# A fused attention and two-layer kernel on one core: another order of the work around the seven products for x w_in

## The chip, the core and the metric

The kernel runs on one core of a Trainium2 chip. The metric is the device time of one execution in microseconds; a kernel's time is the median of its runs. The core has a matrix engine (TensorE, PE in the profile, with its weight loads as PEld), a vector engine (DVE), a scalar engine (ACT), GpSimd (POOL) and SyncE (SP), which here issues all DMA transfers. Each engine works through its own instructions in the order in which the program emits them, and waits on semaphores for the others.

## The reference

Three parts follow each other. q, k, v have 4 batches, 8 heads, 576 rows, 64 columns; the token matrix x that leaves the first part is 2304 x 512, and the weights are 64-bit numbers.

```python
kv = einsum('bhsd,bhse->bhde', k, v)
out = einsum('bhsd,bhde->bhse', q, kv)
x = out / sqrt(mean(out * out, -1) + 1e-6) * g_norm      # as tokens x 512
h = x @ w_in                                             # 512 x 2048
x = (h * sigmoid(h)) @ w_out                             # 2048 x 512
result = ((x @ w_a) * (x @ w_b)) @ w_out2                # 512 x 1536, twice; 1536 x 512
```

## The kernel before, in words

**Tiling.** The 2304 tokens are six blocks j of 384 (TB). A float32 value is held as a high and a low part, and a product is made as three matmuls (high by high, low by high, high by low). w_in and w_out are split into sixteen pieces s of 128 of the inner dimension. PSUM tiles have tags: "h" and "at" with two buffers each, "acc" with four. In SBUF, 37 buffers of 4 KB per partition have the tag "page" and hold weights, raw weights, k and v, and much else; a tile takes a page once an earlier one has had its last use, and a transfer into it waits for that use.

**Steps.** After a start written out by hand (ORDER) the work goes in steps g. VISITS lists which block passes which pieces; base[] is the step at which each visit begins: 0, 4, 12, 20, 28, 32, 48, 64, 80. Steps 4 to 63 are step1: twelve matmuls h = x w_in of one piece (L345), the gate on ACT, its split into gh (ACT) and gl (DVE), then x1_mm, twelve matmuls with w_out (L371) for the step *before*. Blocks 2 and 3 run in steps 32 to 63.

**Work hung on steps.** at(g, f) puts f behind x1_mm of step g, at(-g, f) puts it ahead of those; early[g] puts it between the gate's gh and gl. So the order on every engine is written out through these numbers. On steps 4 to 25 the Decoder turns 64-bit w_in and w_out into high and low parts, with a second key in steps 6 and 9 (EXTRA). Hung on steps are further: sums(u), which makes the additional matrices for the seven products (add, split, store in three steps) and stores them to hsd and hcd; attention of later blocks; combine, which does the same for the x blocks; prepare, which decodes w_a and w_b, forms sums and stores them to wd (twelve calls n, two for each pair p of pieces); and loads.

**Attention items.** For block j and head pair p: load_q_blocks (4 DMAs, 8 where the block crosses a batch, as block 4 does), turn_q (DVE transposes into qT), attend (matmuls ao on PE, squares on ACT, sum on DVE, power on POOL), norm_mul (DVE, xn), and stage_d or stage_f (PE transposes xtp, copies). load_kv and kv_pair make kvc for a batch and a head pair (matmuls kvps). kvps, ao and xtp all use tag "at".

**Units.** From step 64 on, blocks 4 and 5 pass x w_in together: unit u handles pieces 2u and 2u+1 by seven products of six matmuls (L649, Strassen's scheme; banks X, Y, V, Z; the seventh accumulates into Z, so DVE must have read the fifth), with x1_mm calls after products 3 and 6. The first unit has only one x1_mm to do. hooks[k] hold what follows product k+1: what was hung on step 64 + 2u comes at hook 3, on the next step at hook 6; load_unit fetches the matrices of later units (hw 0 to 3 from hsd and hcd). Then sixteen steps (80 to 95) do x1_mm for block 5, during which load_x and load_pairs fetch the transformed x (xc) and the first pairs of w_a, w_b matrices (wp) and raw w_out2. Then eighteen calls of products (seven products with w_a, seven with w_b) alternate with out_mm (L825). decode_out decodes w_out2 in six small parts. load_pairs loads in a fixed order as long as fewer than 21 (NLIVE) matrices are live.

## Time and profile before

| | us |
|---|---|
| median of 3 runs | 893.66 (892.92 to 896.52) |
| profiled execution, its time | 892.13 |
| its span, first to last instruction | 890.3 |
| mean granted TensorE clock | 0.994 |

The profile comes from one execution. Busy time of an engine is the time in which it executed; matmuls are pipelined and their ends modelled. A granted clock of 1.00 is the higher of TensorE's two levels (2.4 GHz), 0.50 the lower (1.2 GHz). A row in a timeline ends with the idle time of the engine before it and with what ended that idle time.

### The profile page before, as it was taken

The numbers are of one execution on the slowest core, as the hardware profiler recorded it, in microseconds if no ns is written. First come the engines' busy times: TensorE is split into PE (matmuls) and PEld (weight loads), VectorE is DVE, ScalarE is ACT, GpSimd is POOL, SyncE is SP. The second block draws the span as 40 slices with busy tenths as digits, with TensorE's granted clock in tenths as the row PEclk, the third lists the DMA queues.
The fourth block names the chain that finished last, engine by engine and source line by source line (L and its number), as shares of the span: only waits on it lengthen the run. The fifth ranks groups of instructions, "written<-read, shape, count | busy, mean of one in ns | idle before, by whom it ended". The sixth has DMA issues, their size and how long they took to land.

```text
span 890.3 us, 13591 instructions
## 1 busy us (share of the span) xinstructions
PE 864.0 (97%) x5014; PEld 819.2 (92%) x5015; DVE 606.1 (68%) x1153; ACT 330.5 (37%) x670; POOL 52.0 (6%) x53
## 2 busy tenths in 40 slices
PE   8999999999999999999989999999999999999998
PEld 5799999999889999999979999999999999999996
DVE  4878998757576786757533878886556665545555
ACT  4766654445254554344422433321131211131110
POOL 4410002001111100000000000000000000000000
PEclk9999999999999999999989999999999999999999
DMA  9950974856885379987599699497777567765001
GB/s 282 376 206 1 276 254 143 264 170 232 251 238 167 140 278 327 340 293 272 213 421 420 269 326 351 151 343 284 272 267 262 179 223 286 266 227 193 1 1 71
DMA packets 124930, 212.19 MB, mean 238 GB/s; under 512 B 41280, under 2 KB 85824, under 8 KB 124864
## 3 DMA queue, kind: packets, MB, share of 16 engines
q1 hardware_dynamic: 124864, 211.33, 67.4%
q8 instruction: 39, 0.64, 0.3%
q14 instruction: 27, 0.22, 0.1%
HBM read 143.92 MB, written 67.37 MB: 237 GB/s over the span
## 4 chain that ended last, share of the span: by engine, by line
PE 78%; DMA 10%; DVE 5%; ACT 2%; issue 1%; SPq 1%; POOL 0%; ACTq 0%; DVEq 0%
PE op L825 17%; PE x1p L371 14%; PE hp L345 11%; PE Z_b L649 4%; PE V_b L649 4%; PE X_b L649 4%; DMA wp<-wd 4%; PE Z_a L649 4%; PE X_a L649 4%; PE V_a L649 4%; PE Y_b L649 2%; PE Y_a L649 2%; PE Z_h L649 2%; DMA hw<-hsd 2%; PE V_h L649 2%; PE X_h L649 2%
## 5 line engine op out<-in xcount | busy, mean ns | idle before, releaser
L371 PE MATMUL x1p<-gh,wo 128*128 128x384 f32 x768 | 197.1, 340 | 4.8 <-ACT gh L355 4.8
L371 PEld LDWEIGHTS x1p<-gh,wo 128*128 128x128 f32 x768 | 140.8, 191 | 5.4 <-ACT gh L355 5.4
L371 PE MATMUL x1p<-gl,wo 128*128 128x384 f32 x384 | 129.5, 341 | 0.4 <-DVE gl L360 0.3
L345 PE MATMUL hp<-xh,wi 128*128 128x384 f32 x512 | 103.5, 343 | 0.4 <-ACT xh L252 0.3
L345 PEld LDWEIGHTS hp<-xh,wi 128*128 128x128 f32 x512 | 88.3, 188 | 1.4 <-ACT xh L252 1.0
L360 DVE TENSOR_TENSOR gl<-g,gh 128x384 fp32r<-128x384 f32 x96 | 54.2, 566 | 46.1 <-ACT gh L355 45.7
L825 PE MATMUL op<-wp,ab 128*128 128x512 f32 x360 | 83.4, 390 | 0.0
L825 PEld LDWEIGHTS op<-wp,ab 128*128 128x128 f32 x360 | 67.5, 188 | 13.6
L706 ACT CAST ab<-a 128x384 fp32r<-128x384 f32 x72 | 37.0, 514 | 115.0 <-DVE a L700 58.3
L371 PEld LDWEIGHTS x1p<-gl,wo 128*128 128x128 f32 x384 | 73.2, 191 | 1.6 <-DVE gl L360 1.6
L833 DVE TENSOR_TENSOR o<-op,o 128x512 f32<-128x512 f32 x90 | 60.5, 686 | 16.6 <-PE op L825 16.6
L825 PE MATMUL op<-w,ab 128*128 128x512 f32 x288 | 66.9, 390 | 0.0
L825 PEld LDWEIGHTS op<-w,ab 128*128 128x128 f32 x288 | 54.0, 188 | 10.9
L355 ACT CAST gh<-g 128x384 fp32r<-128x384 f32 x96 | 49.3, 513 | 22.9 <-PE x1p L371 20.6
L409 ACT ACTIVATE g<-hp 128x384 f32<-128x384 f32 x64 | 31.3, 489 | 67.9 <-PE hp L345 67.9
L345 PE MATMUL hp<-xl,wi 128*128 128x384 f32 x256 | 55.1, 335 | 0.0
L230 POOL TENSOR_TENSOR rr<-ss,nhalf 128x6 f32<-128x6 f32 x24 | 35.8, 1494 | 228.9 <-DVE ss L225 228.9
L345 PEld LDWEIGHTS hp<-xl,wi 128*128 128x128 f32 x256 | 45.3, 188 | 0.3 <-DVE xl L256 0.3
L649 PE MATMUL Z_a<-xc,wp 128*128 128x384 f32 x216 | 43.5, 336 | 1.9 <-DMA xc<-xcd 1.7
L649 PE MATMUL X_a<-xc,wp 128*128 128x384 f32 x216 | 43.7, 337 | 0.0
L649 PE MATMUL Z_b<-xc,wp 128*128 128x384 f32 x216 | 43.3, 335 | 0.0
L649 PE MATMUL V_a<-xc,wp 128*128 128x384 f32 x216 | 43.3, 335 | 0.0
(177 smaller groups left out, 1425.0 us busy)
## 6 DMA issues: line engine op xcount, KB each, us to landing
wp<-wd SPq DMA_DIRECT2D x114, 512.0 KB, 6.7
xc<-xcd SPq DMA_DIRECT2D x21, 768.0 KB, 8.9
hw<-hsd SPq DMA_DIRECT2D x24, 512.0 KB, 6.7
raw_wi<-in_moe_w_in_dram SPq DMA_DIRECT2D x16, 512.0 KB, 8.1
raw_wo<-in_moe_w_out_dram SPq DMA_DIRECT2D x16, 512.0 KB, 7.0
hsd<-hs SPq DMA_DIRECT2D x16, 512.0 KB, 3.8
raw_wa<-in_moe_w_a_dram SPq DMA_DIRECT2D x12, 512.0 KB, 6.3
wd<-s_wa SPq DMA_DIRECT2D x12, 512.0 KB, 3.8
```

Of the source, the lines that this page charges most:

```text
L230: nc.gpsimd.tensor_tensor(r, rms[j, p], nhalf, op=ALU.pow)
L345: nc.tensor.matmul(o, w[wp][:, kt * P:(kt + 1) * P], x[key][:, kt, :], start=(n == 0), stop=(n == 3 * KD - 1))
L355: nc.scalar.copy(gh, src)
L360: nc.vector.tensor_sub(gl, src, gh.bitcast(F32))
L371: nc.tensor.matmul(acc[vi][c], w[wp][:, c * P:(c + 1) * P], gg[vi, s][g], start=(s == s0 and i == 0), stop=(s == s1 - 1 and i == 2))
L409: nc.scalar.activation(g, o, AF.Silu)
L649: nc.tensor.matmul(b[bank], w(name, wq, kt), x(i, xq, kt), start=(fresh and k == 0), stop=(k == 5), skip_group_check=True)
L706: nc.scalar.copy(o[:, 0], t)
L825: nc.tensor.matmul(o, ab[d, p, f, n][:, g, ts], wp[p, 7 + f][:, wq * DM:(wq + 1) * DM], start=(k == 0), stop=(k == 5))
L833: nc.vector.tensor_add(t, o, t)
```

## The change

**Attention.** The items of blocks 3, 4 and 5 come as one list with g0 = 33, 35, ..., 55: block 3 first (four items), then blocks 4 and 5 by turns. Each has load_q_blocks at g0-5, kv load at g0-2 and kv_pair at g0 (not for block 5), turn_q at g0, attend at g0+1, norm_mul ahead of the rest at g0+2, stage_d or stage_f at g0+3. Before, block 3 stood at a pitch of three (34, 37, 40, 43), blocks 4 and 5 at 45, 46, 48, 49, 51, 52, 54, 55. The loads kvt go from steps 32 and 43 to 30 and 38.

**prepare.** Four parts become six: scale (ACT), first_half and second_half (joins on DVE, second also ACT's cast of a), add (stores a, then four sums), high (three ACT casts), low (three DVE subtractions and stores). Calls 0 to 5 begin at steps 36, 42, 48, 54, 58 and 62 with loads three steps ahead, and use side and early places by turns; calls 6 to 11 are spread over the hooks after products 1, 3, 4 and 7 of the units, one part for each, five places apart, loads three places ahead. What call 5 has left over goes to the first three such places.

**Loads and decoding.** decode_out of pair 0 moves from steps 92 and 93 into the first products call (its first half for one piece, its second half for the other). load_pairs takes one load at step 87 and three at each of steps 93 to 95, where it took two at each of 87 to 95. sums(u) begin at 8, 12, 15, 18, 25, 26, 28, 29, before at 11, 14, 17, 20, 24, 26, 28, 30, and store with four DMAs in place of six. combine of blocks 4 and 5 begins one step earlier for kt = 0.

```diff
@@ -262,7 +262,7 @@
         stage_d3(j, p)
 
 
-    raws, mids, W = {}, {}, {}
+    raws, mids, W, wt_ = {}, {}, {}, {}
     srcs = {"wi": w_in, "wo": w_out, "wa": w_a, "wb": w_b, "w2": w_out2}
 
     def load_w(key):
@@ -320,7 +320,7 @@
         dec_sign(key)
 
     def dec_high(key):
-        w = page([P, 2, DM], F32R, f"{key[0]}_{key[1]}")
+        w = wt_[key] = page([P, 2, DM], F32R, f"{key[0]}_{key[1]}")
         nc.scalar.copy(w[:, 0], mids[key])
         W[key] = w[:, 0], w[:, 1]
 
@@ -506,17 +506,20 @@
             for f in wait.pop(0):
                 f()
 
-        def step0():
+        def scale():
             dec_scale(keys[0])
             dec_scale(keys[1])
+
+        def first_half():
             decode(0)
 
-        def step1():
+        def second_half():
             o = page([P, 2, DM], F32R, f"a_{kind}{p}")
             hi(o[:, 0], o[:, 1], m[0], (wd[p, (0, 4)[mat]], flat(o)))
             decode(1)
 
-        def step2():
+        def add():
+            rest()
             for h in range(2):
                 s.append(page([P, 2, DM], F32R, f"s_{h}_{kind}{p}"))
             a11, a12, a21, a22 = (e[:, h * H2:(h + 1) * H2] for e in m for h in range(2))
@@ -525,18 +528,19 @@
             nc.vector.tensor_sub(s3, a11, a21)
             nc.vector.tensor_sub(s2, s1, a11)
             nc.vector.tensor_sub(s4, a12, s2)
-            rest()
-
-        def step3():
+
+        def high():
             a21, a22 = m[1][:, 0:H2].bitcast(F32R), m[1][:, H2:]
             for h in range(2):
                 o = s[h]
                 hi(o[:, 0], o[:, 1], o[:, 1].bitcast(F32), (wd[p, ((1, 2), (5, 6))[mat][h]], flat(o)))
             hi(a21, a22.bitcast(F32R), a22, (wd[p, 3, :, mat * DM:(mat + 1) * DM], m[1].bitcast(F32R)))
+
+        def low():
             for _ in range(3):
                 rest()
 
-        return load, [step0, step1, step2, step3]
+        return load, [scale, first_half, second_half, add, high, low]
 
     w2raw = []
     stores = []
@@ -675,7 +679,7 @@
     PLACES = {"mid": 6, "sig": 2, "gh": 2, "gl": 2}
     ab = {}
 
-    def products(d, p, after=None, more=()):
+    def products(d, p, after=None, more=(), more_b=()):
 
         a = {}
         for n, got in enumerate(seven_ab(d, p, 0, "mid")):
@@ -691,24 +695,26 @@
             if 1 <= n <= len(more):
                 more[n - 1]()
         low = None
-        for got in seven_ab(d, p, 1, "sig"):
+        for n, got in enumerate(seven_ab(d, p, 1, "sig")):
+            if 1 <= n <= len(more_b):
+                more_b[n - 1]()
             if got is None:
                 continue
-            f, n, z, u = got
-            t = a[f, n]
+            f, i, z, u = got
+            t = a[f, i]
             if u is None:
                 nc.vector.tensor_mul(t, z, t)
             else:
-                c = sb.tile([P, TB], F32, tag=("gh", "gl")[f], bufs=2, name=f"b_{d}_{p}_{f}{n}")
+                c = sb.tile([P, TB], F32, tag=("gh", "gl")[f], bufs=2, name=f"b_{d}_{p}_{f}{i}")
                 nc.vector.tensor_add(c, z, u)
                 nc.vector.tensor_mul(t, c, t)
-            o = page([P, 2, TB], F32R, f"ab_{d}_{p}_{f}{n}")
+            o = page([P, 2, TB], F32R, f"ab_{d}_{p}_{f}{i}")
             nc.scalar.copy(o[:, 0], t)
 
             if low:
                 low()
             low = lambda t=t, o=o: nc.vector.tensor_sub(o[:, 1], t, o[:, 0].bitcast(F32))
-            ab[d, p, f, n] = o
+            ab[d, p, f, i] = o
         low()
 
     def sums(u):
@@ -733,9 +739,8 @@
                 nc.vector.tensor_sub(t[:, 1], t[:, 1].bitcast(F32), t[:, 0].bitcast(F32))
 
         def store():
-            for q in range(2):
-                nc.sync.dma_start(hsd[u, 0, :, q * DM:(q + 1) * DM], w0[q].bitcast(F32))
-                nc.sync.dma_start(hcd[u // 2, :, u % 2, q], w1_[q][:, H2:].bitcast(F32))
+            nc.sync.dma_start(hsd[u, 0], wt_["wi", 2 * u].rearrange("p i f -> p (i f)").bitcast(F32))
+            nc.sync.dma_start(hcd[u // 2, :, u % 2], wt_["wi", 2 * u + 1][:, :, H2:].bitcast(F32))
             for h in range(2):
                 nc.sync.dma_start(hsd[u, 1 + h], s[h].rearrange("p i f -> p (i f)").bitcast(F32))
 
@@ -867,26 +872,14 @@
         stage_b(j, p)
         norm_head(j, p)
 
-    for b, g0, pairs in ((2, base[5], (0, 1, 2, 3)), (3, base[5] + 11, (0, 2, 1, 3))):
-        at(g0, load_kvt, b)
-        for i, p in enumerate(pairs):
-            at(g0 + 3 * i, load_kv, b, p)
-            at(g0 + 2 + 3 * i, kv_pair, b, p)
-
     v4 = base[4]
     for p in range(NP):
         at(v4 - 9 + 2 * p, turn_q, 2, p)
         at(v4 - 8 + 2 * p, attend, 2, p)
         at(-(v4 - 7 + 2 * p), norm_mul, 2, p)
         at(v4 + p // 2, stage_d, 2, p)
-    for p in range(NP):
-        at(-(base[5] + 4 + 3 * p), norm_mul, 3, p)
-        at(base[5] + 2 + 3 * p, turn_q, 3, p)
-        at(base[5] + 3 + 3 * p, attend, 3, p)
-        at(base[5] + 5 + 3 * p, stage_d, 3, p)
     for i in range(4):
         at(v4 - 13 + i, load_q_blocks, 2, i)
-        at(base[5] - 4 + i, load_q_blocks, 3, i)
 
     def stage_f(j, p):
         if j not in xf:
@@ -894,23 +887,46 @@
         stage_d1(j, p)
         nc.scalar.activation(xf[j][:, p, :], xt.pop((j, p)), AF.Copy, scale=g2)
 
-    for i, (p, j) in enumerate([(p, j) for p in (0, 2, 1, 3) for j in (4, 5)]):
-        g0 = base[5] + 13 + i * 3 // 2
-        at(g0 - 4, load_q_blocks, j, p)
+    at(base[5] - 2, load_kvt, 2)
+    at(base[5] + 6, load_kvt, 3)
+    for i, (p, j) in enumerate([(p, 3) for p in range(NP)] + [(p, j) for p in (0, 2, 1, 3) for j in (4, 5)]):
+        g0 = base[5] + 1 + 2 * i
+        if j != 5:
+            b = 2 if j == 3 else 3
+            at(g0 - 2, load_kv, b, p)
+            at(g0, kv_pair, b, p)
+        at(g0 - 5, load_q_blocks, j, p)
         at(g0, turn_q, j, p)
         at(g0 + 1, attend, j, p)
         at(-(g0 + 2), norm_mul, j, p)
-        at(g0 + 3, stage_f, j, p)
-
-
-
-    early = {}
+        at(g0 + 3, stage_d if j == 3 else stage_f, j, p)
+
+    early, inner = {}, {}
+
+    def at_unit(h, fn):
+        inner.setdefault(h, []).append(fn)
+
     for n in range(2 * NPAIR):
         load, steps = prepare(("wa", "wb")[n % 2], n // 2)
-        g0 = base[5] + (1, 6, 11, 16, 20, 24, 28, 31, 34, 37, 40, 43)[n]
-        at(g0, load)
-        for i, f in enumerate(steps):
-            at(g0 + 2 + i, f)
+        if n < 6:
+            g0 = base[5] + (4, 10, 16, 22, 26, 30)[n]
+            at(g0 - 3, load)
+            for i, f in enumerate(steps):
+                g = g0 + (i + 1) // 2
+                if g >= base[7]:
+                    at_unit(i - 3, f)
+                elif i % 2 == 0:
+                    at(g, f)
+                else:
+                    early.setdefault(g, []).append(f)
+        else:
+            h0 = 1 + 5 * (n - 6)
+            if n == 6:
+                at(base[6] + 15, load)
+            else:
+                at_unit(h0 - 3, load)
+            for i, f in enumerate(steps):
+                at_unit(h0 + i, f)
     todo = [f for kt in range(2) for f in combine(0, kt, mid)]
     for n, fs in enumerate(todo):
         for f in fs:
@@ -926,7 +942,7 @@
         made[u][0]()
 
     for u in range(NF1 // 2):
-        g0 = (11, 14, 17, 20, 24, 26, 28, 30)[u]
+        g0 = (8, 12, 15, 18, 25, 26, 28, 29)[u]
         at(g0, begin_sums, u)
         at(g0 + 1, lambda u: made[u][1](), u)
         at(g0 + 2, lambda u: made[u][2](), u)
@@ -950,7 +966,7 @@
                 f()
 
         for n in range(12):
-            at(base[6] + (5, 11)[kt] + n * 5 // 12, parts, n)
+            at(base[6] + (4, 11)[kt] + n * 5 // 12, parts, n)
     for n, (u, i) in enumerate(((0, 0), (0, 3), (0, 1), (0, 2), (1, 1))):
         at(base[6] + 10 + n, load_unit, u, i)
     gs = base[8]
@@ -958,6 +974,7 @@
     at(gs, load_x, 0, 0)
     for s in (0, 1, 3, 5):
         at(gs + s, load_pairs, 2)
+    at(gs + 7, load_pairs, 1)
     at(gs + 4, load_x, 0, 1)
     at(gs + 6, load_x, 0, 2)
 
@@ -970,15 +987,8 @@
     at(gs + 2, change)
     at(gs + 9, load_x, 0, 5)
     at(gs + 13, load_x, 0, 6)
-    for s in range(7, NF1):
-        at(gs + s, load_pairs, 2)
-
-    def all_of(make, *args):
-        for f in make(*args):
-            f()
-
-    for f in range(2):
-        at(gs + 12 + f, all_of, decode_out, 0, f)
+    for s in range(13, NF1):
+        at(gs + s, load_pairs, 3)
 
     halves = []
 
@@ -1161,6 +1171,8 @@
             hooks = {n: [] for n in range(7)}
             hooks[0] += left
             left = []
+            for h, k in enumerate((0, 2, 3, 6)):
+                hooks[k] += inner.get(4 * u + h, [])
             hooks[3] += both(g)
             hooks[6] += both(g + 1)
             for n, to, i in (((0, 1, 0), (0, 1, 2)) if u == 0 else ()) + (
@@ -1194,7 +1206,7 @@
                     late[kt] = combine(d + 1, kt, half_page, late.pop("blocks"))
                 todo = late[kt][6 * h:6 * h + 6]
             products(d, p, (lambda: x1_mm(*prev)) if n == 0 else None,
-                     decode_out(p, 0) if new else [])
+                     decode_out(p, 0) if n < NPAIR else [], decode_out(p, 1) if n == 0 else [])
             if n % NPAIR == NPAIR - 1 and n + 1 < len(seq):
                 for i in range(7):
                     load_x(d + 1, i)
```

## Rows read from the trace of the kernel before

**Rows 1.** The page, busy time of each engine (share of the span), and its DMA issues.

```profile
PE 864.0 (97%) x5014; PEld 819.2 (92%) x5015; DVE 606.1 (68%) x1153; ACT 330.5 (37%) x670; POOL 52.0 (6%) x53
...
wp<-wd SPq DMA_DIRECT2D x114, 512.0 KB, 6.7
```

**Rows 2.** Windows, columns: stretch, its length, busy time (x instructions) of each engine, PEclk, DMA share, GB/s.

```profile
116.00:131.20 15.20, 14.25 (x86) 13.64 (x85) 15.01 (x31) 8.10 (x16) 1.64 (x1) 1.00 0.70 231
171.50:232.80 61.30, 61.30 (x426) 60.03 (x426) 41.66 (x85) 28.70 (x63) 5.58 (x4) 1.00 0.66 215
232.80:330.74 97.94, 93.45 (x623) 89.92 (x621) 66.44 (x134) 49.46 (x103) 12.42 (x9) 1.00 0.66 212
330.74:344.71 13.97, 11.52 (x56) 10.91 (x55) 8.09 (x17) 3.46 (x8) 0.00 (x0) 0.88 0.88 346
344.71:356.19 11.48, 11.48 (x68) 11.48 (x67) 8.62 (x16) 7.22 (x15) 0.00 (x0) 1.00 1.00 325
356.19:369.35 13.16, 11.76 (x68) 11.44 (x67) 8.84 (x18) 5.19 (x11) 0.00 (x0) 1.00 0.87 331
392.31:405.45 13.14, 11.74 (x68) 11.42 (x67) 8.84 (x18) 5.18 (x11) 0.00 (x0) 1.00 0.75 281
428.57:471.31 42.74, 38.37 (x205) 37.41 (x205) 19.08 (x36) 13.21 (x26) 0.00 (x0) 0.92 0.91 362
471.31:504.98 33.67, 31.91 (x182) 31.30 (x182) 19.23 (x36) 8.01 (x16) 0.00 (x0) 1.00 1.00 405
```

**Rows 3.** The waits of PE over the span: total us, times, longest.

```profile
PE xtp L248 <- DVE xn L235: 3.0, 4, 1.2
...
PE ao L214 <- DVE qT L153: 0.8, 1, 0.8
```

**Rows 4.** Timeline, attention: start, us, instruction [idle before <-releaser].

```profile
221.66 3.86 SPq L145 DMA_DIRECT2D qb<-in_q_dram  x8
...
238.54 0.69 PE L180 MATMUL kvps<-kv 128*64 128x64 f32 x16 [1.31 <-DMA kv<-in_v_dram]
...
244.79 0.66 ACT L296 ACTIVATE m_wa<-raw_wa 128x512 f32<-128x512 f32 x1 [5.20 <-DMA raw_wa<-in_moe_w_a_dram]
...
289.54 0.55 DVE L235 TENSOR_TENSOR xn<-ao,rr 128x384 f32<-128x384 f32 x1
...
290.15 0.55 PE L248 MATMUL xtp<-ident,xn 128*128 128x128 f32 x3 [0.87 <-DVE xn L235]
```

**Rows 5.** Timeline, end of step 63 and the units.

```profile
321.11 0.32 SPq L430 DMA_DIRECT2D wd<-a_wb  x1
...
324.97 1.41 SPq L749 DMA_DIRECT2D hw<-hsd  x2
...
335.43 1.30 PE L649 MATMUL V_h<-hT_None,hw 128*128 128x384 f32 x6 [2.41 <-DMA hw<-hsd]
...
364.24 1.29 DVE L429 TENSOR_TENSOR s_wb<-s_wb 128x512 fp32r<-128x512 f32 x2 [3.63 <-ACT s_wb L428]
...
367.57 0.55 DVE L787 TENSOR_TENSOR h<-Z_h,u_h 128x384 f32<-128x384 f32 x1
...
368.18 1.33 PE L649 MATMUL Z_h<-hB_None,hw 128*128 128x384 f32 x6 [1.40 <-DVE h L787]
```

**Rows 6.** Timeline, sixteen steps after the units and first products call.

```profile
460.92 0.66 ACT L562 ACTIVATE m_w<-raw_w 128x512 f32<-128x512 f32 x1 [4.23 <-DMA raw_w<-in_moe_w_out_dram]
...
464.61 1.01 PE L371 MATMUL x1p<-gh,wo 128*128 128x384 f32 x2 [4.11 <-ACT gh L355]
...
481.56 1.28 PE L649 MATMUL Z_a<-xc,wp 128*128 128x384 f32 x6 [1.75 <-DMA xc<-xcd]
```

**Rows 7.** Groups by line, one call of prepare: xcount | busy us, mean ns.

```profile
L308 DVE SCALAR_TENSOR_TENSOR m_wb<-raw_wb,m_wb 128x512 uint32<-128x512 uint32 x12 | 8.3, 692 | 0.4
...
L524 DVE TENSOR_TENSOR s_wb<-m_wb 128x256 f32<-128x256 f32 x6 | 2.5, 414 | 0.0
...
L428 ACT CAST s_wb<-s_wb 128x512 fp32r<-128x512 f32 x12 | 6.8, 617 | 0.0
```

## The prediction

> **What bounds the kernel now.** I read the busy line of the page first: of a span of 890.3 us TensorE (PE) is busy 864.0, VectorE (DVE) 606.1, ScalarE (ACT) 330.5 [rows 1]. So only PE's own time counts, and an edit to other engines can give back at most what PE loses by waiting. Then the windows by stage [rows 2], to see where it is lost. One unit of the x w_in stage with nothing in its way takes 11.48 us for 66 matmuls by the code (42 of the seven products, 24 of two x1_mm), 0.174 us each. I hold the other stretches against that pace:
> - steps 32 to 44 (171.5 to 232.8): PE busy 61.30 of 61.30, nothing lost, although attention items of block 3 run in it;
> - from step 45 to the end of step 63 (232.8 to 330.74): 97.94 us with 93.45 busy, 4.49 idle;
> - units 2 and 5: 13.16 and 13.14, so 1.68 and 1.66 over; unit 0 has one x1_mm less (54 matmuls, 9.40 us) and took 13.97, 4.57 over, its clock on average 0.88;
> - the sixteen steps after the units (428.57 to 471.31): 205 matmuls, 35.67 us at the pace, took 42.74: 7.07 over, with a granted clock of 0.92; the first two products calls (471.31 to 504.98): 182 matmuls, 31.67, took 33.67: 2.00 over;
> - around step 22 (116.0 to 131.2): 15.20 with 14.25 busy, 0.95 idle.
> Together 22.4 us. Outside these stretches the rows leave next to nothing that order could give.
>
> By the Trainium skill (page Perfetto Trace Analysis, Identifying the Most-Contended Engine) matmul busy time is a bad measure of headroom and LDWEIGHTS busy time a better one. Here that line says 819.2 of 890.3 [rows 1], 71 us of room instead of 26. The trace sides with the matmuls: the products call stretch spends 31.30 of 33.67 on weight loads while its DMA wait alone explains 1.75 of the difference [rows 2, 6], and a sum made by the 71 would promise three times what waits cost.
>
> **The change part by part.**
>
> *Attention at an even pitch.* Nothing is computed more or less; the twelve items of blocks 3 to 5 start every second step (33 to 55) in place of every third, then two in three. Three waits make up the 4.49. (1) The transposes xtp waited for DVE's xn four times, 3.0 us in all [rows 3]. In one of them the xn that ended at 290.09 released a matmul at 290.15 [rows 4]; by the code that xn belongs to the *next* item (its own norm_mul ran a step earlier), so PE waited for the buffer: ao, kvps and xtp share two PSUM buffers ("at"), and in a step with a kv_pair, a stage_f and another item's norm_mul all three meet. At pitch two, norm_mul of item i-1 and kv_pair of item i fall into the odd step, xtp of i-1 and ao of i into the even one, so each buffer is given up a whole step (about 4.2 us, 24 matmuls) before it is asked for. (2) kvps waited 1.31 for a load of k and v [rows 4]. SP issues in order, and eight q-block issues just ahead took 3.86 [rows 4]; an item of block 4 makes eight, blocks 3 and 5 four, and the new order puts at least two steps between them. The load itself keeps its lead of two steps. (3) ACT stood 5.20 us at the scaling of a raw w_a [rows 4], and the gates behind it in ACT's queue held x1_mm; raws are now loaded three steps before they are scaled, not two. I take back the 4.49. Steps 32 to 44 show that such items can run with no idle time. The far ends: nothing, and 4.49 times 7.07 / 4.37 = 7.3, since in the stage after the units the loss at the pace was 7.07 where idle time was 42.74 - 38.37 = 4.37.
>
> *w_a and w_b in six parts.* The same instructions (per call on DVE seven at 0.69 and seven at 0.41 to 0.42, 7.8 us [rows 7]), but high (three ACT casts) and low (three DVE subtractions and the stores) are now one place apart, and so are scaling and joining. In unit 2, after product 4, the old last part of one call met the first part of the next: DVE idled 3.63 for ACT's cast, subtracted, joined, and the h that frees bank Z ended at 368.12; PE idled 1.40 for it [rows 5]. Unit 5 has the same two parts in the same place. In the new order no place in units 1 to 7 has more than 2.4 us of DVE work (add: one at 0.69, four at 0.41), and its inputs are a place old; between the h of product 5 and the seventh product lie 18 matmuls, 3.1 us. I take back 1.68 + 1.66.
> Unit 0's 4.57 came from hw, loaded behind the store of a_wb: the store was issued at 321.11, the last hw load behind it at 324.97, and V_h started at 335.43 after 2.41 us of idling [rows 5]; the clock fell after it. That was call six, whose store stood in step 60. In the new order call six reaches its stores in unit 0, and at this point stand those of call five, at the head of steps 60 and 61, with their data a step old: hw 1 and 2 leave about a step (4.2 us) sooner, more than the 2.41. What is late next is in the same unit: add, high and low of the sixth call and scale and first_half of the seventh all come in its first three hooks, and with a single x1_mm the seventh product follows the sixth. ACT: the copy of x1's third group ends at about 5.4 us (27 matmuls, 4.7, and the copy), then three casts of at most 0.62 [rows 7] and one scaling of 0.66 [rows 4]; DVE: 0.41 + 0.69 + 0.69, then h 0.55: 10.3 us, against 48 matmuls, 8.35; I take off 0.4 because ends of neighbours overlap and one cast is half as wide. I take 1.5 for it, between 0 and the 4.57 of today. So this part gives 1.68 + 1.66 + 4.57 - 1.5 = 6.4.
>
> *decode_out moved, loads held back.* ACT waited 4.23 us for raw w2 at the end of a full DMA queue, and gh of the next step came late: PE idled 4.11 [rows 6], and the stage's clock averages 0.92 [rows 2]. The decoding now goes into the first products call, which began at 471.31 when the raw, even in the old order, was there at 460.92. Pair 1's nine loads move from steps 87 to 95 to steps 93 to 95, out of the way of the last xc, which the first call awaited for 1.75 [rows 6]. I take back 7.07 + 2.00. What is paid: four DVE operations (0.42 + 3 x 0.69 = 2.5) in the second half of the first call, which has 13 operations of 0.55, 7.2 us of the 7.3 that 42 matmuls take; the overrun of 2.4 meets the next half (five, plus its own 2.5: 5.3 of 7.3). Between 0 and 2.4; I take 0.6, as most of it is absorbed. Net 8.5.
>
> The Trainium skill speaks against holding loads back (page DMA: Bandwidth & Descriptors, Rules for kernel authors: issue the DMA early, wait late). The nine loads of 512 KB [rows 1] are 4.7 MB, 11.7 us at the 405 GB/s of that stretch [rows 2]; from step 93 to the second call lie three steps of 2.1 and a call of 16.8, 23 us. By the rule the second call would wait, and this part give less, once the queue still holds more than 11 us of other loads at step 93; with one xc in front I keep the 8.5.
>
> *Sums of w_in.* Eight times two adds of 512 columns, four of 256 and two subtractions, 4.4 us of DVE [rows 7], moved by up to three steps; the fourth goes from step 20 to 18. In step 22 ao waited 0.8 for DVE's qT [rows 3]; at 20 the sums met the first attention of block 2. That 0.95 goes; sums at 8 and 9 now meet the doubled decoding of step 9. I take 0.5, between 0.95 gained and 0.95 lost. The stores drop from six issues to four per unit; SP is not waited for there: nothing.
>
> **The sum.** 4.5 + 6.4 + 8.5 + 0.5 = 19.9. The profiled execution took 892.13 with a span of 890.3; it becomes 872.2. The median of the three runs is 893.66, 1.53 above, so the forecast is 873.8.
>
> **Rivals.**
> (a) *Attention waits in another place*: SP, now with even more kinds of loads between the stores of step 33 to 44, reaches k and v late; 1.31 at each of eight pairs, 10.5 us: 884.3. For it: SP's order, not the load, was late in today's wait [rows 4]. Against: fewer q-block issues in one step.
> (b) *The stage after the units is bound by its bytes, not its order*: then waits for raw w2 and xc become waits for pair 1 and 8.5 is not gained: 882.3. For it: DMA share 0.91 and 1.00 there [rows 2]. Against: by the code nine pair loads, not twenty, stand ahead of the last xc.
> (c) *Slower*: pages. 37 buffers hold w_out, the split x and hw, and a call's six parts hold theirs longer. SP waits for a page in front of hw, as it stood behind a_wb at 321.11; the load of 324.97 was used 10.5 us later and was late. hw for unit u+2 has little more than one unit, 11.48. If raws and stores in front push it past that, each of units 1 to 7 loses what unit 0 lost, 4.57: 32 us, 905.8; from five units on (22.9) it is slower than before. For it: the stores of low now stand right in front of hw's loads. Against: they waited there already, with longer DVE chains. The Trainium skill says that DMA engines wait for no semaphore and the issuing sequencer does (DMA: Bandwidth & Descriptors, Anatomy of one DMA); that is this mechanism.
> (d) *Nearly nothing*: two of these at once, 889 to 898.
>
> **Chances.** Forecast 0.56 (869 to 878), (a) 0.12, (b) 0.12, (d) 0.10, (c) 0.10. A measurement of this kernel tells about 0.5% from no change, 4.5 us. Faster by more 0.80, within 0.10, slower 0.10. Low end: all 22.4, and attention's 7.3 for 4.5, without what is paid back: 893.66 - 25.2 = 868.5. The high end takes in (a) and (b): 884.3.
>
> **What would show it.** Right: in the trace after, no xtp waiting for xn; units 1 to 7 at 11.5 each and unit 0 between 9.4 and 11; the steps after the units at 2.1 each with the clock at 1.00; the second half of the first products call with DVE busy throughout. Wrong: kvps waiting for k and v in steps 33 to 55 (a), Z_a or X_a of the second call waiting for wp (b), hw waits in several units (c).

## The result and the profile after

| | before | after |
|---|---|---|
| median of the runs, us | 893.29 (4 runs, 891.72 to 896.52) | 882.26 (4 runs, 879.19 to 884.84) |
| profiled execution, us | 892.13 | 884.84 |
| its span, us | 890.3 | 883.0 |

The change gives back 11.0 us where 19.9 were forecast, a ratio of 0.987 (95% interval 0.983 to 0.991). That lies inside the stated range. The four runs of after lie 5.65 us apart, and the traced one is the slowest of them; the section on the hardware comes back to that.

The page's busy line of after stands beside [rows 1]. Of the 7.3 us by which the traced span is shorter, 2.6 are busy time of TensorE and 4.7 idle time. Busy time shrinks where the clock is back up: the steps after the units had 38.37 busy at a granted clock of 0.92 [rows 2] and have 35.20 at 1.00 (fifth row below).

```profile
PE 861.4 (98%) x5015; PEld 818.0 (93%) x5015; DVE 604.3 (68%) x1153; ACT 330.7 (37%) x670; POOL 51.9 (6%) x53
```

I cut both traces at the same places of the program, by the first matmul of a step, unit or products call. The last column is the change of the forecast for this stretch.

| stretch | before | after | difference | forecast |
|---|---|---|---|---|
| start up to step 4 | 48.55 | 49.93 | +1.4 | 0 |
| steps 4 to 32 (sums) | 127.10 | 127.46 | +0.4 | -0.5 |
| steps 33 to 44 | 57.17 | 68.79 | +11.6 | |
| steps 45 to 63 | 97.91 | 90.50 | -7.4 | |
| both together (attention) | 155.09 | 159.29 | +4.2 | -4.5 |
| units 0 to 6 | 86.19 | 81.40 | -4.8 | -6.4 |
| unit 7 and sixteen steps | 54.38 | 46.84 | -7.5 | |
| first two products calls | 41.72 | 40.83 | -0.9 | |
| both together | 96.10 | 87.67 | -8.4 | -8.5 |
| the rest | 377.30 | 377.29 | 0 | 0 |

The start is code that the change does not touch, and in the other kernels below step 4 began anywhere between 48.4 and 50.2. So of the four terms of the sum one is right to 0.1 (the stage after the units), one is 1.6 too large (the units), one is small and of the wrong sign (the sums), and attention is off by 8.7, with the wrong sign. The windows of after, with the columns of [rows 2]:

```profile
177.39:246.18 68.79, 64.34 (x442) 61.30 (x442) 39.29 (x81) 26.54 (x59) 8.47 (x6) 0.95 0.64 196
246.18:336.68 90.50, 89.75 (x583) 87.35 (x582) 60.09 (x122) 47.41 (x99) 10.73 (x7) 1.00 0.63 205
336.68:347.81 11.13, 9.69 (x56) 9.37 (x56) 10.58 (x22) 5.58 (x12) 0.00 (x0) 1.00 0.77 292
359.29:372.04 12.75, 11.71 (x68) 11.42 (x67) 9.01 (x18) 5.82 (x12) 0.00 (x0) 1.00 1.04 408
429.72:464.92 35.20, 35.20 (x205) 35.20 (x205) 12.42 (x23) 9.59 (x19) 0.00 (x0) 1.00 0.95 381
464.92:481.98 17.06, 16.95 (x98) 16.63 (x97) 10.90 (x21) 5.26 (x11) 0.00 (x0) 1.00 1.02 418
481.98:505.75 23.77, 23.05 (x121) 21.29 (x121) 19.78 (x39) 11.03 (x23) 0.00 (x0) 1.00 0.84 341
```

Steps 45 to 63 (second row) now have 0.75 idle instead of 4.49; two attention items have also left them for steps 41 to 44. The steps after the units (fifth row) run at the pace with no idle time and a full clock. And steps 33 to 44 (first row), which had none before, now idle 68.79 - 64.34 = 4.45 at a granted clock of 0.95. TensorE's waits in that stretch (total, times, longest):

```profile
PE kvps L180 <- DMA kv<-in_v_dram: 2.6, 1, 2.6
PE ao L214 <- DVE qT L153: 1.5, 2, 0.8
PE x1p L371 <- DVE gl L360: 0.3, 1, 0.3
```

How the waits for qT come about stands in the timeline of steps 35 to 37 of after (columns as in [rows 4]):

```profile
192.66 0.23 DVE L190 COPY kvc<-kvps 64x64 f32<-64x64 f32 x1 [0.84 <-ACT kvc L186]
...
196.57 0.49 PE L248 MATMUL xtp<-ident,xn 128*128 128x128 f32 x3
...
197.10 0.58 DVE L153 STREAM_TRANSPOSE qT<-qb 128x384 f32<-128x384 f32 x1 [4.22 <-PE xtp L248]
...
197.82 0.91 PE L214 MATMUL ao<-kvc,qT 128*128 128x128 f32 x6 [0.76 <-DVE qT L153]
...
198.15 0.34 SPq L430 DMA_DIRECT2D xcd<-x  x1
...
198.77 0.51 ACT L428 CAST hT<-T 128x384 fp32r<-128x384 f32 x1 [6.14 <-PE ao L214]
```

VectorE stands for 4.22 us ahead of qT, an operation that reads only q. It is released by the transposes xtp of the item *before*, the last work but one in TensorE's step. qT needs no result of xtp; it needs a place to write. ScalarE stands 6.14 at hT, an operation of the combining of blocks 0 and 1, until ao has read qT; and SyncE, which issues in order, sends the store of that combining only at 198.15. Six steps later the same happens again (4.25 at qT), and just ahead of it stands the dearer wait:

```profile
219.71 1.19 SPq L114 DMA_DIRECT2D kv<-in_k_dram  x1
...
220.95 0.85 SPq L114 DMA_DIRECT2D kv<-in_v_dram  x1
...
226.64 1.12 PE L180 MATMUL kvps<-kv 128*64 128x64 f32 x16 [2.64 <-DMA kv<-in_v_dram]
...
227.91 2.93 PE L345 MATMUL hp<-xh,wi 128*128 128x384 f32 x8
...
229.94 0.56 DVE L235 TENSOR_TENSOR xn<-ao,rr 128x384 f32<-128x384 f32 x1 [6.35 <-DMA xcd<-hB]
```

A load of k and v that the order puts at step 39 is issued in step 41, TensorE waits 2.64 for it, the clock falls, and eight matmuls take 2.93 instead of the 1.63 of other steps.

The buffers explain the waits at qT. qT, xn and most tiles of combine come from one tag, "mid", with six buffers. The addresses in the built program of after give, in the order of allocation:

```
tile    T1  qT(3,0)  hT1  hT3  T2  hB22  xn(3,0)  qT(3,1)  hT2
buffer   0     4      2    3   1    4       5        5       5
```

When qT of the second item is allocated, all six are taken, and it gets the buffer of the xn that stands just ahead of it and that xtp reads a step later; hT2 gets it next. With the old pitch two combining tiles and a step lie between xn(3,0) and qT(3,1), and qT gets another buffer.

### The profile page after: what moved, and what is told of

Its sections match the earlier page's. It is cut to its first block, busy times and chain, and to the rows that moved or that the text cites. A ratio compares the mean times of both kernels' runs of the same rounds, so it can differ in the third digit from the quotient of the medians.

```text
span 883.0 us, 13575 instructions
## 1 busy us (share of the span) xinstructions
PE 861.4 (98%) x5015; PEld 818.0 (93%) x5015; DVE 604.3 (68%) x1153; ACT 330.7 (37%) x670; POOL 51.9 (6%) x53
## 4 chain that ended last, share of the span: by engine, by line
PE 84%; DVE 7%; DMA 4%; SPq 2%; issue 2%; ACT 1%; POOL 0%; DVEq 0%; POOLq 0%; ACTq 0%
PE x1p L371 19%; PE op L830 17%; PE hp L345 12%; PE Z_a L653 4%; PE V_b L653 4%; PE X_b L653 4%; PE Z_b L653 4%; PE X_a L653 4%; PE V_a L653 4%; PE Y_b L653 2%; PE Y_a L653 2%; PE Z_h L653 2%; DMA kvt<-in_v_dram 2%; PE V_h L653 2%; PE X_h L653 1%
## 5 line engine op out<-in xcount | busy, mean ns | idle before, releaser
L371 PE MATMUL x1p<-gh,wo 128*128 128x384 f32 x768 | 193.9, 335 | 0.0
L371 PEld LDWEIGHTS x1p<-gh,wo 128*128 128x128 f32 x768 | 138.9, 188 | 0.0
L653 PE MATMUL V_b<-xc,wp 128*128 128x384 f32 x216 | 43.3, 335 | 0.0
```

The lines of the kernel that those rows point to most:

```text
L371: nc.tensor.matmul(acc[vi][c], w[wp][:, c * P:(c + 1) * P], gg[vi, s][g], start=(s == s0 and i == 0), stop=(s == s1 - 1 and i == 2))
L653: nc.tensor.matmul(b[bank], w(name, wq, kt), x(i, xq, kt), start=(fresh and k == 0), stop=(k == 5), skip_group_check=True)
```

## Experiments

Theory A says that the stall in steps 33 to 44 is these six buffers. Its rivals: the six parts of prepare (B), SyncE's order (S, the prediction's rival (a)), and, further on, pages (P) and bytes (D). The ratios in brackets are to the kernel before, run beside each group.

**att_old: the attention lists as they were, all else changed.**

```diff
-    for i, (p, j) in enumerate([(p, 3) for p in range(NP)] + [(p, j) for p in (0, 2, 1, 3) for j in (4, 5)]):
-        g0 = base[5] + 1 + 2 * i
...
+    for p in range(NP):
...
+        at(base[5] + 2 + 3 * p, turn_q, 3, p)
...
+    for i, (p, j) in enumerate([(p, j) for p in (0, 2, 1, 3) for j in (4, 5)]):
+        g0 = base[5] + 13 + i * 3 // 2
```

> The changed kernel with its attention lists put back as they were before (block 3 at a pitch of three steps, blocks 4 and 5 at 45 to 55, kvt loads at 32 and 43); everything else as changed. Theory A (buffers): at pitch two the items of block 3 and the combining of blocks 0 and 1 want more than the six buffers of the tag mid, so VectorE stands at qT until the transposes at the end of the next step have read the buffer. Then steps 33 to 44 lose nothing here, the waits after step 45 come back in part (3 to 4.5 us), and the time is 876 to 880. Theory B (the stall comes from the six parts of prepare, not from the pitch): 4 to 5 us of idle time stay in steps 33 to 44, and the time is 883 to 887.

Measured: 874.52 (0.979, 0.977 to 0.981), 7.7 faster than the whole change. The windows of steps 45 to 63 and 33 to 44 of this kernel, and its only attention wait in either:

```profile
233.29:326.42 93.13, 92.66 (x622) 89.87 (x621) 62.85 (x128) 48.15 (x100) 12.90 (x9) 1.00 0.64 209
176.05:233.29 57.24, 57.24 (x402) 55.88 (x402) 36.42 (x75) 26.60 (x57) 5.73 (x4) 1.00 0.66 211
...
PE xtp L248 <- DVE xn L235: 0.5, 1, 0.5
```

Theory B falls: with prepare's six parts in place, steps 33 to 44 lose nothing. But theory A had also expected the waits after step 45 to come back in part, 876 to 880, and they stay away at the old pitch. The pitch was not what they needed.

**prep_back: att_old with prepare in four parts at the old places too.**

```diff
...
-            g0 = base[5] + (4, 10, 16, 22, 26, 30)[n]
-            at(g0 - 3, load)
...
+        g0 = base[5] + (1, 6, 11, 16, 20, 24, 28, 31, 34, 37, 40, 43)[n]
+        at(g0, load)
+        for i, f in enumerate(steps):
+            at(g0 + 2 + i, f)
```

> The kernel of att_old (changed kernel, attention lists as before the change) with prepare put back as well: four parts at the old places, loads two steps ahead. Left of the change are the held loads, the moved decoding and the sums. If, as the prediction has it, the six parts are worth only what the units gained (4.8 in the trace) and the pitch cured steps 45 to 63, att_old could not have been free of waits there; the kernel then is 874.5 + 4.8 = 879 to 880. If it is the six parts with raws three steps ahead that cured steps 45 to 63, the 4.49 comes back as well: 874.5 + 4.8 + 4.5 = 883 to 885, with transposes waiting for xn again.

Measured: 884.87 (0.990, 0.987 to 0.994), 10.35 slower than att_old. The waits of TensorE and ScalarE in its steps 45 to 63 (total, times, longest):

```profile
PE kvps L180 <- DMA kv<-in_v_dram: 3.1, 2, 2.3
PE xtp L248 <- DVE xn L235: 2.3, 3, 1.0
...
ACT m_wa L296 <- DMA raw_wa<-in_moe_w_a_dram: 7.0, 4, 4.5
...
ACT m_wb L296 <- DMA raw_wb<-in_moe_w_b_dram: 2.1, 2, 1.2
```

The waits of [rows 3, 4] are back, and with them 9.1 us in which ScalarE stands for raw w_a and w_b. In att_old and in after ScalarE does not wait for a raw in this stretch at all. So prepare's order is worth about 10 us by the medians. In the traces 5.3 of it lie in units 0 to 6 (86.53 against 81.27) and 7.4 in steps 33 to 63 (157.73 against 150.37); the second number is large because the traced execution of prep_back, 888.11, is its slowest. Whether there it is the raws three steps ahead or the six parts was not taken apart.

**pitch_alone: the kernel before with the new attention lists alone.**

```diff
...
+    for i, (p, j) in enumerate([(p, 3) for p in range(NP)] + [(p, j) for p in (0, 2, 1, 3) for j in (4, 5)]):
+        g0 = base[5] + 1 + 2 * i
...
```

> The kernel before with the attention lists of the change alone (pitch of two steps, kvt loads at 30 and 38). By the prediction's step it gives back 4.49: 889. If the pitch itself brings the stall at the six buffers of tag mid, and the waits after step 45 were prepare's, steps 33 to 44 lose 4 to 9 and nothing or only a part of the 4.49 comes back: 893 to 900.

Measured: 896.22 (1.004, 1.001 to 1.006): slower by about 3. Its window of steps 33 to 44, and, in steps 45 to 63, TensorE's only wait of some size and ScalarE's waits for raws:

```profile
176.18:242.81 66.63, 62.49 (x442) 60.14 (x442) 43.32 (x89) 27.87 (x62) 8.52 (x6) 0.97 0.66 205
...
PE x1p L371 <- ACT gh L355: 1.3, 1, 1.3
...
ACT m_wb L296 <- DMA raw_wb<-in_moe_w_b_dram: 7.0, 4, 3.4
ACT m_wa L296 <- DMA raw_wa<-in_moe_w_a_dram: 6.4, 4, 2.8
```

No xtp waits for xn after step 45 and no kvps for k and v, so what the prediction's steps (1) and (2) promised did happen; that it comes from parting the three users of the tag "at" is read from the code. ScalarE still stands 13.4 us for raws here, so that wait alone does not stop xtp or kvps. But 4.14 of idle time has appeared in steps 33 to 44, here with the old prepare. The pitch brings its own stall. Steps 33 to 63 of before, att_old, pitch_alone and after side by side show why the two edits did not add up:

| | old prepare | six parts |
|---|---|---|
| old pitch | 155.09 (157.73 in prep_back) | 150.37 |
| pitch of two | 157.91 | 159.29 (157.4 and 157.2 in dec_back and pairs_back below) |

Either edit removes nearly all of the waits after step 45; the second one has nothing left to remove there, and the pitch's price in steps 33 to 44 remains.

**qt_page: qT of blocks 3 to 5 in the pages, order as changed.**

```diff
-        qT[j, p] = mid([P, TB], F32, f"qT_{j}_{p}")
+        qT[j, p] = (page if j > 2 else mid)([P, TB], F32, f"qT_{j}_{p}")
```

> The changed kernel with qT of blocks 3 to 5 in the 4 KB pages instead of the six buffers of the tag mid; order, loads and pitch as changed. Theory A (buffers): VectorE's two waits of 4.2 us at qT go, the stores of the combining leave in time, and with them the loads of k and v; steps 33 to 44 have under 1 us of idle time at a full clock: 873 to 877. Theory S (SyncE's queue): the waits at qT go, but k and v are still waited for by 2 us or more: 879 to 882.

Measured: 878.31 (0.983, 0.981 to 0.985), 4.0 faster than after, just between the two expectations. VectorE's two waits of 4.2 at qT are gone, step 36 takes 5.19 instead of 6.18, and step 41 6.05 instead of 8.31. Steps 41 to 43 together take 19.80 instead of 21.43, but 19.49 and 19.35 in dec_back and pairs_back below, which have the attention of after. Three rows of its steps 41 and 42:

```profile
218.02 0.82 SPq L114 DMA_DIRECT2D kv<-in_v_dram  x1
...
221.99 0.69 PE L180 MATMUL kvps<-kv 128*64 128x64 f32 x16 [0.92 <-DMA kv<-in_v_dram]
...
228.04 0.56 DVE L235 TENSOR_TENSOR xn<-ao,rr 128x384 f32<-128x384 f32 x1 [7.38 <-DMA xcd<-hB]
```

xn still shares the six buffers, and waits for the store of the combining's hB to leave one of them.

**qt_xn_page: xn of block 3 in the pages as well.**

```diff
-        xn[j, p] = mid([P, CH, 2, D], F32, f"xn_{j}_{p}")
+        xn[j, p] = (page if j == 3 else mid)([P, CH, 2, D], F32, f"xn_{j}_{p}")
```

> The kernel of qt_page with xn of block 3 in the pages too, so that no attention item of steps 33 to 41 shares buffers with the combining of blocks 0 and 1. Theory A (buffers): what was left in qt_page, an xn that waits 7.4 us for the store of the combining's hB to land, goes too; steps 33 to 44 keep under 1 us of idle time: 874 to 876. Theory P (pages): ten pages more are held in these steps, SyncE waits for pages in front of k, v or the raws, and the time is 877 or more.

Measured: 876.56 (0.982, 0.979 to 0.985): 5.7 faster than after, and near the border of A and P. VectorE no longer waits at the six buffers, and one wait for k and v is left, with a fall of the clock behind it. Two rows of its timeline, and SyncE's wait for a page just before them:

```profile
218.00 0.95 SPq L114 DMA_DIRECT2D kv<-in_v_dram  x1
...
223.52 1.12 PE L180 MATMUL kvps<-kv 128*64 128x64 f32 x16 [2.46 <-DMA kv<-in_v_dram]
...
SPq L122 <- PE kvps L180: 2.8, 1, 2.8
```

So A is one cause, shown by taking the shared buffers away: 4.0 and 5.7 of the 7.7 between after and att_old, by the medians. It is not the cause of the late load of k and v. In after, qt_page and qt_xn_page alike SyncE stands 2.8 at kvt until a page is free, and issues the first half of that load 0.1 to 0.2 after the first matmul of step 41, whether VectorE stood at the six buffers or not. What differs is the time from the issue of its second half to the matmul that waits for it: 5.7, 4.0 and 5.5, with waits of 2.64, 0.92 and 2.46. Why the load takes that long there is open; in att_old TensorE does not wait for it. How much of A's gain lies in steps 33 to 44 is open too: they take 65.60 and 66.02 in these two traces, 68.79 in after, and 66.89 and 66.74 in dec_back and pairs_back.

**kv4: each load of k and v four steps ahead.**

```diff
-            at(g0 - 2, load_kv, b, p)
+            at(g0 - 4, load_kv, b, p)
```

> The changed kernel with each load of k and v four steps ahead of its use instead of two. Theory S (SyncE's queue: the load is issued too late, as in rival (a) of the prediction): the wait of 2.6 us for k and v in step 41 goes and with it the fall of the clock, some 6 us: 875 to 877. Theory A (buffers): VectorE still stands twice for 4.2 us at qT until the transposes of the item before, TensorE still waits 0.76 for qT twice, and what SyncE issues behind the stores of the combining stays late: 879 to 882.

Measured: 897.19 (1.005, 1.003 to 1.007): 15 slower than after, outside both expectations. SyncE's, VectorE's and TensorE's longest waits in steps 32 to 45:

```profile
SPq L122 <- PE kvps L180: 21.4, 2, 17.0
...
DVE xn L235 <- DMA xcd<-hB: 16.1, 2, 10.4
...
PE kvps L180 <- DMA kvt<-in_v_dram: 4.0, 1, 4.0
```

The earlier loads hold the pages longer, SyncE stands 17 us at the page of kvt with all stores and loads behind it, and TensorE loses 4 to 5.5 at a time. This is the mechanism of the prediction's rival (c), in another place than it named. The Trainium skill's rule to issue a DMA early and wait late (DMA: Bandwidth & Descriptors, Rules for kernel authors) did not pay here, where the buffer of the load was not free: two steps earlier cost 15 us.

**kv_first: qt_xn_page, with the first k, v load of block 4 one step earlier and kvt of its batch two later.**

```diff
-    at(base[5] + 6, load_kvt, 3)
+    at(base[5] + 8, load_kvt, 3)
...
-            at(g0 - 2, load_kv, b, p)
+            at(g0 - 2 - (b == 3 and p == 0), load_kv, b, p)
```

> The kernel of qt_xn_page with two entries of SyncE's queue moved: the load of k and v for the first item of block 4 one step earlier, ahead of the stores of prepare's first call, and the load of the last rows of block 3's batch (kvt) two steps later, so that SyncE doesn't stand at its page in front of the others. Theory S (what is left of the stall is SyncE's order, rival (a) of the prediction): the wait for k and v of 2.46 us in step 41 goes and the clock stays up: 872 to 874. Theory D (the bytes in steps 39 to 42 are too many in any order): another load is waited for by 1.5 us or more there, 875 to 878.

Measured: 881.29 (0.987, 0.985 to 0.989), 4.7 slower than qt_xn_page and outside both expectations. k and v are there now, kvt is not:

```profile
PE kvps L180 <- DMA kvt<-in_v_dram: 5.1, 1, 5.1
```

Behind the stores of prepare and two raws, kvt landed 6.0 us after its issue. So this edit only trades one late load for another. That some other order fits (S) or that none does (D) is not shown.

**dec_back: the decoding of w_out2 back in steps 92 and 93.**

```diff
+    for f in range(2):
+        at(gs + 12 + f, all_of, decode_out, 0, f)
...
-                     decode_out(p, 0) if n < NPAIR else [], decode_out(p, 1) if n == 0 else [])
+                     decode_out(p, 0) if new else [])
```

> The changed kernel with the decoding of w_out2 of pair 0 back in steps 92 and 93, the pair loads held back as changed. If the move of the decoding is what freed the stage after the units: ScalarE waits about 4 us for raw w2 again, TensorE 4 us for gh, the clock falls there, and the time is 887 to 890. If holding the pair loads back does it alone (raw w2 then no longer stands at the end of a full queue): no wait there, the first products call gets its 0.9 us of overrun back, and the time is 881 to 883.

Measured: 882.93 (0.988, 0.986 to 0.991), no difference from after that can be told. ScalarE's wait for raw w2 and TensorE's for the gate in the stage after the units:

```profile
ACT m_w L566 <- DMA raw_w<-in_moe_w_out_dram: 0.4, 1, 0.4
...
PE x1p L371 <- ACT gh L355: 1.2, 2, 0.8
```

With the pair loads held back raw w2 is late by 0.4 and not by 4.23 [rows 6]. In the trace unit 7 and the sixteen steps take 2.6 more than in after and the first two products calls 1.1 less, so moving the decoding was worth at most 1.5 of the 8.4.

**pairs_back: load_pairs two per step from 87 to 95, the decoding moved.**

```diff
-    at(gs + 7, load_pairs, 1)
+    at(gs + 7, load_pairs, 2)
...
-    for s in range(13, NF1):
-        at(gs + s, load_pairs, 3)
+    for s in range(8, NF1):
+        at(gs + s, load_pairs, 2)
```

> The changed kernel with load_pairs at two loads per step from step 87 to 95 again, the decoding moved as changed. By the prediction both the raw w2 at the end of the queue and the last xc are then late again, but with the decoding out of the steps no gate waits for raw w2: only the xc wait of 1.75 in the first products call comes back, 883 to 885. If the full queue itself is what the stage suffered from (other waits behind it), 887 to 890.

Measured: 886.94 (0.994, 0.992 to 0.996), 4.7 slower than after, where the two expectations meet. The sixteen steps are as fast as in after, but the first products call takes 24.18 instead of 17.06:

```profile
475.93 2.26 PE L653 MATMUL Z_a<-xc,wp 128*128 128x384 f32 x6 [4.87 <-DMA xc<-xcd]
...
462.56:486.74 24.18, 19.20 (x98) 18.59 (x98) 10.88 (x21) 5.26 (x11) 0.00 (x0) 0.86 1.02 417
```

Since nothing stops TensorE in the steps any more, it comes to the last xc earlier and waits for it longer, 4.87 instead of 1.75 [rows 6], and the clock falls to 0.86 there. Moving the decoding alone only moves the wait; holding the loads back removes it, with the decoding at either place. Against the Trainium skill's rule that the prediction weighed (the one named at kv4), the later issue is the faster one; the queue carried 417 GB/s in this call and 418 in that of after.

**old_n7: att_old with two parts of the eighth call, and its loads, one place earlier.**

```diff
-                at_unit(h0 - 3, load)
+                at_unit(h0 - 3 - (n == 7), load)
...
-                at_unit(h0 + i, f)
+                at_unit(h0 + i - (n == 7 and i < 2), f)
```

> The kernel of att_old with scale and first_half of the eighth call of prepare one place earlier, so that first_half and second_half don't lie one product apart (end of unit 1 and first product of unit 2). If those two, 3.6 us of VectorE's time within one product and the start of the next three, are why V_h waits in unit 2: unit 2 takes 11.5 instead of 12.5, the kernel 873 to 874; but low of the seventh call now meets first_half in unit 1, and if that is as bad, unit 1 takes 12 to 12.5 and the time doesn't change (874 to 875).

Measured: 874.43 (0.979, 0.978 to 0.981), the same as att_old, and unit 2 takes 12.87, no less. My reason for unit 2 falls. In att_old the profile names another releaser for its wait:

```profile
357.26 1.29 PE L653 MATMUL V_h<-hT_None,hw 128*128 128x384 f32 x6 [0.76 <-DMA hw<-hcd]
```

That load was issued at 347.33 and took 9.8 us in a full queue. In after the same load landed 0.14 us ahead of the V_h of unit 2, while its row names VectorE's h, which ended at about the same time.

**old_1246: att_old with prepare's places after products 2, 3, 5 and 7.**

```diff
-            for h, k in enumerate((0, 2, 3, 6)):
+            for h, k in enumerate((1, 2, 4, 6)):
```

> The kernel of att_old with prepare's places in the units after products 2, 3, 5 and 7 instead of 1, 3, 4 and 7, more evenly apart. If the wait of the seventh product in unit 0 (1.44) and of V_h in unit 2 (0.8 to 1.0) come from two places one product apart: both go, units 0 and 2 take about 9.8 and 11.5, the kernel 871.5 to 873. If VectorE's work in front of the h of product 5 matters in itself: another unit waits instead, 874 to 876.

Measured: 874.85 (0.980, 0.978 to 0.982). Unit 0 takes 9.42 instead of 11.14, its pace, but unit 1 takes 14.60 instead of 11.48 and unit 2 13.06.

**best: att_old, those places in unit 0 alone, and the load of hcd after product 3.**

```diff
+            for h, k in enumerate((1, 2, 4, 6) if u == 0 else (0, 2, 3, 6)):
...
-                    (3, u + 2, 0), (4, u + 2, 1), (6, u + 2, 2)) + (((5, u + 1, 3),) if u % 2 else ()):
+                    (3, u + 2, 0), (4, u + 2, 1), (6, u + 2, 2)) + (((2, u + 1, 3),) if u % 2 else ()):
```

> The kernel of att_old with two more edits: in unit 0 alone prepare's places come after products 2, 3, 5 and 7 (in old_1246 unit 0 then took 9.42 instead of 11.14), and in odd units the load of the next pair's last matrix (hcd) is issued after product 3, not 6 (in att_old it landed 0.14 us ahead of the V_h of units 2 and 4 that wanted it, 9.8 us after its issue). If unit 0's wait is VectorE's order and unit 2's is this load, unit 0 takes 9.4, unit 2 and 4 take 11.5, and the kernel 874.5 - 1.7 - 1.0 = 871.5 to 872.5. If the load's page isn't free earlier, SyncE stands there, other loads come late, and units 1 to 5 lose 1 us or more: 873.5 to 877.

Measured: 875.11 (0.981, 0.978 to 0.985), not better than att_old. Units 2 and 4 take 11.48 each now, so the load was their cause, 1.25 together. Unit 0 takes 9.42, and unit 1 14.77. The windows of units 0 and 1 of best, and below the dots those of att_old:

```profile
326.45:335.87 9.42, 9.42 (x56) 9.42 (x55) 7.08 (x16) 5.22 (x11) 0.00 (x0) 1.00 0.75 279
335.87:350.64 14.77, 12.04 (x68) 11.40 (x68) 12.42 (x25) 7.41 (x15) 0.00 (x0) 1.00 0.99 357
...
326.42:337.56 11.14, 9.70 (x56) 9.38 (x55) 10.59 (x22) 5.58 (x12) 0.00 (x0) 1.00 0.78 292
337.56:349.04 11.48, 11.48 (x68) 11.48 (x67) 8.84 (x18) 7.30 (x15) 0.00 (x0) 1.00 1.03 358
```

VectorE's busy time in the two units is 19.50 in best and 19.43 in att_old: unit 0's wait was paid later, with interest. att_old without the places but with the earlier load would be some 1.2 faster by these rows; it was not run. The fastest kernels of the study are att_old and old_n7 at 874.5.

## Why the prediction was right or wrong

The time lies inside the range by luck as much as by working. The forecast's own bounds, 869 to 878, were missed. The range reached 882.26 only because its high end took in rivals (a) and (b); (b) did not come, and (a) came at one load instead of eight. Most of what is missing from the forecast is a price of the new pitch that stood in no term.

**The stage after the units: right.** Forecast 8.5, measured 8.4. The clock is back at 1.00 and no gate waits. Rival (b) falls: the DMA share is 0.95 in the steps, which have no idle time at all (fifth row). The price of the moved decoding, taken at 0.6, is there as well: in the trace after, VectorE works through the second half of the first call, and in the next call the fourth product, X_a, waits for u_a.

```profile
485.99 1.31 PE L653 MATMUL X_a<-xc,wp 128*128 128x384 f32 x6 [0.72 <-ACT u_a L658]
```

What the working had not seen is which of the two edits does it. I treated them as two causes, 7.07 and 2.00. dec_back and pairs_back show one main cause, nine loads ahead of everything that is needed sooner; the decoding is at most 1.5 of it.

**prepare in the units: right in kind, 1.6 too large.** Unit 5 runs at the pace. Unit 0 kept a wait of 1.44 against the 1.5 taken for it, at the place that was named, the seventh product behind VectorE's add, high and low:

```profile
346.05 0.55 DVE L792 TENSOR_TENSOR h<-Z_h,u_h 128x384 f32<-128x384 f32 x1
...
346.65 1.31 PE L653 MATMUL Z_h<-hB_None,hw 128*128 128x384 f32 x6 [1.44 <-DVE h L792]
```

Its floor was the working's 9.40, and 11.13 came out, 0.13 above "between 9.4 and 11". Unit 2 kept 1.27 of its 1.68, which had been taken back whole. The wait of 1.40 at the seventh product [rows 5] is gone, and the sixth waits 1.04 instead, by best for the load of hcd. In before that load is issued 2.95 us ahead of unit 2 and lands 0.47 ahead of the sixth product; in after it is issued 1.60 ahead of the unit, with three stores of prepare between 354.83 and 356.30 standing right in front of the hw loads. Rival (c) had named such stores as a reason, but with pages, and 4.57 in each of seven units.

**Attention: the step that failed.** Three parts of it went wrong in different ways.

First, the credit. The 4.49 was put down to the pitch on three waits; in before 2.4 of it are at xtp (the 3.0 of [rows 3] are those of the whole span), 1.3 at kvps and 0.7 at a gate. att_old shows that prepare's new order takes all of it away but 0.5, at the old pitch, and pitch_alone that the pitch takes away all but 1.3 with the old prepare. Sub-step (3), ScalarE standing for the raws, belonged to the part on prepare from the start. Whether it was behind (1) and (2) as well is not shown: in pitch_alone ScalarE waits longer for the raws than in before, 13.4 against 10.2, and (1) and (2) are gone. Two edits had one gain to share, so the sum without the pitch would have been nearly the same. That is why a forecast of 873.8 describes att_old (874.5), a kernel without the pitch, better than the one it was made for.

Second, the price. It was set at nothing with "Steps 32 to 44 show that such items can run with no idle time". They did at a pitch of three. At a pitch of two steps 33 to 63 take 8.9 more in the traces (159.29 against 150.37 in att_old). The number of buffers that the items take from the tag mid, and who else takes from it in these very steps, was not counted: combine takes ten tiles for each kt, the items two each. I counted the two PSUM buffers of the tag "at" and not the six in SBUF. The far end for this edit was "nothing"; the loss of 4.2 against before lay outside the bounds. The six buffers are not the whole price: in the trace TensorE's waits for qT are 1.5 of the 4.45.

Third, rival (a) had the right place and the wrong size. SyncE does come late to k and v in steps 39 to 41, once, at 2.64 us and a fall of the clock, not eight times at 1.31. In front of it stands kvt, put one step ahead of it in the new order and held 2.8 for a page. With 884.3 for that rival the measured 882.26 lies between it and the forecast.

**Sums: wrong, small.** Step 22 still waits, 1.08 us. With the sums out of the way VectorE idles there, and what it waits for is GpSimd's power between ss and xn:

```profile
126.73 0.55 DVE L225 TENSOR_REDUCE ss<-sq 128x6 f32<-128x390 f32 x1
...
129.30 0.56 DVE L235 TENSOR_TENSOR xn<-ao,rr 128x384 f32<-128x384 f32 x1 [1.22 <-POOL rr L230]
...
131.58 0.57 DVE L153 STREAM_TRANSPOSE qT<-qb 128x384 f32<-128x384 f32 x1
```

xn, two joins and a split of the decoding stand ahead of qT in VectorE's order, and all of them are held up by xn. ss itself comes later than before, 0.16 us ahead of the first matmul of step 22 instead of 1.49. In VectorE's order the last subtractions of the sums, 1.25 us, now stand ahead of it, where the working had only looked at what left step 22. Step 11 lost 0.64 to the earlier sums.

## What to carry to other kernels

When work is moved closer together, count the buffers of every tag that it shares with what already runs there, in SBUF as well as in PSUM, from the first write to the last read or the landing of the store. An engine that waits at an operation whose inputs are long there, and is released by another engine's *read*, may be waiting for a buffer; the cure then is another buffer or more distance, not an earlier issue.

Before giving a wait to an edit, ask which other edit of the same change removes it too: two edits that remove the same wait do not add up, and a two-by-two table of kernels shows it in two runs beside before and after.

## What the runs showed of the hardware

One wait of 2 to 3 us in a stretch that otherwise runs through can cost twice its length. In before a wait of 2.41 us for hw went with a granted clock of 0.88 in unit 0, which took 13.97 us against 9.40 at the pace, 4.57 more [rows 2, 5]. In after the 2.64 us for k and v are followed by matmuls at the lower clock: eight hp matmuls take 2.93 us, a step later 1.66, and over steps 33 to 44 a granted clock of 0.95 makes, as an estimate, (1 - 0.95) x 68.79 = 3.4 us beside the 4.45 of idle time. The four executions of after differ in this: granted clocks of 0.995, 0.997, 0.998 and 1.000 go with 884.84, 881.78, 882.74 and 879.19 us, while those of att_old, with no such wait, lie at 0.999 to 1.000 and within 873.87 to 875.32. The traced execution of after is the slowest, so it shows the loss in steps 33 to 44 larger than the median would; dec_back and pairs_back, with the same attention, take 2 us less there.

The same load at the same place of the order took 4.0 to 5.7 us from issue to use (qt_page, qt_xn_page, after), and the matmul behind it waited 0.92 to 2.64.
